# Gated attention and a squared-ReLU layer: w1 and the first inputs fetched by SyncE and GpSimd, half of the partitions each

## The chip, the cores and the metric

The kernel runs on one core of a Trainium2 chip. The metric is the device time of one execution in microseconds (us). A core has five engines with their own instruction streams: TensorE (PE in the profile; PEld is its weight load), VectorE (DVE), ScalarE (ACT), GpSimd (POOL) and SyncE (SP), which here does nothing but issue transfers. Transfers run on 16 DMA engines, whoever issues them. Before the change, SyncE issued all but six of the transfers of this kernel; those six were issued by ScalarE and none by GpSimd.

## The reference

```
# attention: q, k, v, a_re, a_im of shape (4, 8, 768, 48), f32
mag = sqrt(a_re**2 + a_im**2)
scale = minimum(mag, 0.999) / (mag + 1e-6)
a = (a_re + i a_im) * scale
for t in range(768):
    S = a[t][:, None] * S + outer(k[t], v[t])     # S complex, 48 x 48 for each batch and head
    y[t] = q[t] @ real(S)
# bridge: x = y as (3072 tokens, 384)
h = maximum(x @ w_in, 0)                          # w_in 384 x 2048
out = (h * h) @ w_out                             # w_out 2048 x 384
```

The two weights come as 64-bit floats. The kernel reads them as pairs of 32-bit words and makes 32-bit floats of them itself.

## The kernel before

The 768 steps of a sequence are cut into chunks of 128. A chunk of one sequence holds all 8 heads. Two sequences at the same chunk make a group, so there are 12 groups (0 to 11), six for each pair of sequences. For each group the kernel makes operands (gates, prefix products of the gates, keys and queries scaled by them), does the attention of both sequences with matrix products (`scores`, `sums_of_values`, `added`, `new_state`), brings the result into a token tile `x`, and runs the feed-forward layer over its 256 tokens (`first_product`, `squared_relu`, and the second product).

Features lie on the partitions: the even heads on partitions 0 to 63, the odd ones on 64 to 127, 48 features each. The 16 partitions that are left in each half hold the rows of the last two heads, three features side by side. So each load of q, k and the gates (`load_parts`, L487 to L501) goes half by half: for each of the two sequences and each half `hh` one transfer for the 48 rows (L493) and two or three small ones for the 16 rows (L501). The tile `raw` exists once. A group's load can start when the group before has no more use for it.

A load of a whole group is 16 transfers of 1.5 MB together. Group 0 alone is loaded in two parts: `l0.0` (the gates, 768 KB, half by SyncE and half by ScalarE), and `l0.1` (q and k, 768 KB, all by SyncE). `load_values` (`v`) fetches the values of a group in two transfers, 384 KB together.

The weight w1 is fetched in eight blocks of 256 columns (`fetch`, f0 to f7). A block is 768 KB in six transfers, because `w1_views` sets the rows of w1 to the same crossed order of partitions: in each half of the partitions two transfers for the 48 rows and one for the 16 rows (L617). The blocks of w2 (f8 to f15) are one transfer each (L613). The tile `words` has three buffers, so block i + 3 can't be fetched before block i has been decoded by VectorE (`weights`, D, L577 to L584 and a sum) and checked by ScalarE (`watch`, W, L590 and L592).

The order of all work is written out by hand in one long string, FRONT. A token is a letter and numbers: `l` loads the inputs of a group, `v` its values, `f` fetches a block of a weight, `D` decodes it, `W` checks it, `oG.K` is step K of the operands of group G, `aG.K` and `bG.K` are step K of the attention of its two sequences, `g` fills the rows of the token tile that the last heads belong to, `F`, `H` and the other capitals are the feed-forward layer, `s` stores. Every engine that is named in `by_hand` (L1173) executes its instructions in the order in which the tokens issue them. The string begins:

```
"l0.0 M0 v1 f0 v0 o0.0 l0.1 o0.3 o0.1 o0.4 o0.5 o0.7 o0.2 M1 D0 f1 o0.10 o0.8 o0.9 "
"o0.11 W0 o0.6 o0.12 o0.15 o0.22 f2 W1 o0.13 o0.16 o0.14 l1 W2 o0.17 D1 o0.18 f3 o0.19 "
"o0.20 o1.0 o1.6 a0.1 o1.3 o0.21 o1.1 D2 o1.2 a0.2 f4 a0.3 W3 D3 a0.0 a0.4 o1.4 o1.5 "
```

The operand steps that matter here, in the numbering of the list at L821: 0 `squares` (ACT L684, needs the tile `room`), 3 `sum_of_squares` (DVE L697), 6 `queries` (ACT L669, the first to need the loaded q), 7 `inverse` (DVE L715), 11 `gates` (DVE L735 and L739), 12 `negated` (ACT L743), 13 `grow` (DVE L755), 14 `keys` (ACT, the last to need `raw`), 15 and 16 the steps in blocks (DVE, `pr` and `ab` at L478), 19 `carried` (DVE, uses `room`), 20 `products` (DVE, writes `qk`), 21 `last_heads`. Most of VectorE's sums and products are recorded at L478, since a helper issues them.

`last_heads` copies the rows of the last two heads by six transfers (L815) into the tile `last`, and then GpSimd makes two small products (`prod`, L817 and L818) from it, which `new_state` (step 9 of the attention) uses on VectorE. Apart from the fills of tiles at the very start, these are all that GpSimd does.

Of the kernel before, what the change touches and what calls it, by code (L numbers as in the profile page):

```python
# [23 lines left out]
I32 = mybir.dt.int32  # L24
U32 = mybir.dt.uint32
AF = mybir.ActivationFunctionType
ALU = mybir.AluOpType
PSUM = bass.MemoryType.PSUM

P = 128  # L30
HH = 2
ROWS = 64
# [393 lines left out]
def quotient_path(ctx, tc, feat, vtok, w_in, w_out, w1, w2, out, n_seq, count):  # L426
# [49 lines left out]

    def tt(out, in0, in1, op):
        nc.vector.tensor_tensor(out=out, in0=in0, in1=in1, op=op)  # L478
# [8 lines left out]
    def load_parts(gi, part=None):  # L487

        parts = [slice(A_RE, Q), slice(Q, V), slice(A_RE, V)][2 if part is None else part]
        queues = nc.sync, (nc.scalar if part == 0 else nc.sync)  # L490
        for b, n in enumerate(groups[gi]):
            for hh, queue in enumerate(queues):
                queue.dma_start(  # L493
# [107 lines left out]
    def fetch(i):  # L601
        of_w2, j = block(i)
        f, fbs = slice(j * BLK, (j + 1) * BLK), slice(j * 2, (j + 1) * 2)
        if (w_out if of_w2 else w_in).dtype == F32:
            if of_w2:
                nc.sync.dma_start(out=w2[:, fbs], in_=w2_view(w_out)[:, fbs])
            else:
                for at, gs, src in w1_views(w_in, D, crossed=True):
                    nc.sync.dma_start(out=w1[at, gs, f], in_=src[:, :, f])
            return  # L610
        words = words_of[i] = dec.tile([P, E, 2], I32, name="words", bufs=3)
# [3 lines left out]
        else:  # L615
            for at, gs, src in w1_views(w_in, D, crossed=True):
                nc.sync.dma_start(  # L617
                    out=words[at].rearrange("p (g f) w -> p g (f w)", g=NG)[:, gs],
                    in_=src[:, :, f].bitcast(I32))
# [36 lines left out]
    operands = {}  # L656

    def make_operands(gi):
# [151 lines left out]
        def last_heads():  # L810
            for hh in range(HH):
                for g in range(NG):
# [4 lines left out]
            nc.gpsimd.tensor_copy(out=pd[:, now, :, NG], in_=last[gi % 2][:, 0:2, :, C])  # L817
            nc.gpsimd.tensor_scalar(out=pd[:, 0, :, NG], in0=last[gi % 2][:, IM, :, C], scalar1=-1.0,  # L818
                                    scalar2=None, op0=ALU.mult)
# [10 lines left out]
    def chunk(gi, b):  # L830
# [66 lines left out]
        def added():  # L897
            add = tiles["add"] = pm.tile([P, 2, NP, D], F32, tag="m", name="add")
            for c in (RE, IM):
                for p_ in range(NP):  # L900
                    for hh in range(HH):
                        rr, at = slice(hh * ROWS, (hh + 1) * ROWS), (HH * p_ + hh) * D
                        nc.tensor.matmul(add[rr, c, p_], lhsT=kt[c][:, p_, rr],  # L903
                                         rhs=v[:, at:at + D], start=True, stop=True)

# [114 lines left out]
    def outputs(i, r):  # L1020
# [30 lines left out]
        "l0.0 M0 v1 f0 v0 o0.0 l0.1 o0.3 o0.1 o0.4 o0.5 o0.7 o0.2 M1 D0 f1 o0.10 o0.8 o0.9 "  # L1051
        "o0.11 W0 o0.6 o0.12 o0.15 o0.22 f2 W1 o0.13 o0.16 o0.14 l1 W2 o0.17 D1 o0.18 f3 o0.19 "
        "o0.20 o1.0 o1.6 a0.1 o1.3 o0.21 o1.1 D2 o1.2 a0.2 f4 a0.3 W3 D3 a0.0 a0.4 o1.4 o1.5 "
        "a0.8 a0.5 a0.6 a0.9 a0.7 f5 b0.1 o1.7 W4 b0.0 D4 o1.10 o1.8 o1.9 b0.5 b0.2 b0.3 o1.11 "
        "W5 f6 b0.6 b0.4 b0.8 b0.7 g0 D5 o1.12 o1.22 v2 o1.13 W6 f7 F0.0 o1.15 o1.14 l2 F0.1 "
        "H0.0 o1.16 W7 F0.2 o1.17 H0.1 F0.3 H0.2 f8 D6 o1.18 F0.4 H0.3 o1.19 F0.5 H0.4 o2.6 "
        "F0.6 H0.5 o1.20 o2.0 f9 H0.6 W8 o2.3 o1.21 b0.9 o2.1 a1.1 D7 o2.2 a1.2 a1.3 W9 a1.0 D8 "
        "f10 a1.4 o2.4 o2.5 a1.8 F0.7 a1.5 a1.9 a1.6 H0.7 a1.7 f11 b1.1 D9 b1.0 b1.2 W10 b1.3 "
        "b1.4 b1.5 b1.8 D10 b1.6 b1.7 v3 T0.0 W11 g1 f12 b1.9 T0.1 D11 T0.2 F1.0 o2.7 W12 f13 "
        "D12 F1.1 H1.0 o2.10 F1.2 H1.1 o2.8 F1.3 H1.2 D13 f14 W13 F1.4 H1.3 T0.3 o2.9 o2.11 "  # L1060
        "F1.5 H1.4 f15 W14 D14 F1.6 o2.12 o2.22 T0.4 o2.13 W15 T0.5 o2.15 H1.5 T0.6 o2.14 H1.6 "
        "l3 o2.16 F1.7 T1.0 H1.7 o2.17 T1.1 D15 o2.18 T1.2 o2.19 T1.3 T0.7 o3.6 o2.20 o3.0 T1.4 "
        "E0.0 E0.1 s0.0 s0.1 o3.3 o3.1 a2.1 o2.21 T1.5 t0 o3.4 o3.2 t1 T1.6 o3.5 t2 a2.2 T1.7 "
        "o3.7 o3.10 a2.3 t3 E1.0 E1.1 s1.0 a2.0 o3.8 s1.1 o3.9 a2.5 a2.4 a2.6 o3.11 a2.8 a2.7 "
        "b2.0 a2.9 o3.12 o3.22 b2.1 b2.5 b2.2 b2.6 o3.15 b2.3 b2.7 b2.4 g2 b2.8 v4 o3.16 F2.0 "
        "o3.17 F2.4 H2.0 o3.13 o3.18 F2.1 H2.4 b2.9 o3.14 F2.5 H2.1 l4 X2.0 o3.19 F2.2 H2.5 "
        "F2.6 H2.2 X2.1 o3.20 F2.3 H2.6 F2.7 H2.3 X2.2 o3.21 Y2.0 Y2.1 Y2.2 Z2.0 H2.7 X2.3 o4.0 "
        "Y2.3 a3.1 o4.3 R2.0 Z2.1 o4.6 o4.4 o4.5 b3.0 Q2.2 Q2.1 Q2.3 o4.1 R2.1 Q2.0 o4.7 o4.2 "
        "Z2.2 b3.5 o4.10 o4.8 b3.6 Z2.3 R2.2 b3.7 o4.9 a3.0 o4.11 R2.3 a3.2 a3.3 Z2.4 a3.4 a3.5 "
        "o4.12 o4.22 o4.15 a3.8 a3.6 Z2.5 a3.7 g3 R2.4 o4.16 Z2.6 R2.5 o4.17 s2.0 F3.0 R2.6 "  # L1070
        "s2.1 a3.9 o4.18 F3.4 H3.0 o4.13 b3.1 H3.4 F3.1 b3.2 X3.0 o4.14 Y3.0 b3.3 F3.5 o4.19 "
        "H3.1 l5 b3.4 b3.8 H3.5 F3.2 X3.1 b3.9 F3.6 H3.2 v5 o4.20 F3.3 H3.6 F3.7 H3.3 X3.2 "
        "o4.21 Y3.2 Y3.1 o5.0 a4.1 Z3.0 o5.3 H3.7 X3.3 o5.4 Z3.1 R3.0 Y3.3 o5.6 o5.5 b4.0 Q3.1 "
        "Q3.0 Q3.3 o5.1 R3.1 Q3.2 o5.7 o5.2 Z3.2 a4.2 b4.5 o5.10 a4.3 R3.2 b4.6 a4.4 o5.8 a4.8 "
        "Z3.3 a4.9 b4.7 o5.9 a4.0 o5.11 R3.3 Z3.4 a4.5 o5.12 o5.22 o5.15 a4.6 b4.1 a4.7 Z3.5 "
        "b4.2 g4 R3.4 o5.16 b4.3 Z3.6 b4.4 R3.5 o5.17 s3.0 b4.8 R3.6 s3.1 F4.0 v6 b4.9 o5.18 "
        "F4.4 H4.0 o5.13 F4.1 H4.4 X4.0 o5.14 Y4.0 F4.5 o5.19 H4.1 l6 F4.2 H4.5 X4.1 F4.6 H4.2 "
        "o5.20 F4.3 H4.6 X4.2 o5.21 F4.7 H4.3 Y4.2 Y4.1 Z4.0 H4.7 X4.3 o6.0 Y4.3 b5.0 o6.3 R4.0 "
        "o6.6 o6.4 Z4.1 b5.5 o6.5 o6.7 o6.1 b5.6 o6.2 Q4.1 Z4.2 Q4.0 Q4.3 b5.7 R4.1 Q4.2 o6.10 "
        "o6.8 a5.0 R4.2 o6.9 Z4.3 a5.5 o6.11 a5.6 R4.3 Z4.4 a5.7 v7 o6.12 g5 o6.15 o6.22 Z4.5 "  # L1080
        "R4.4 Z4.6 R4.5 o6.16 s4.0 F5.0 R4.6 s4.1 o6.17 F5.4 H5.0 o6.13 o6.18 F5.1 H5.4 X5.0 "
        "o6.14 Y5.0 F5.5 o6.19 H5.1 l7 F5.2 H5.5 X5.1 F5.6 H5.2 o6.20 F5.3 H5.6 X5.2 o6.21 a6.1 "
        "H5.3 Y5.2 F5.7 Y5.1 a6.2 a6.3 H5.7 Z5.0 X5.3 o7.0 Y5.3 o7.3 a6.4 b6.0 R5.0 o7.4 o7.6 "
        "a6.8 b6.5 Z5.1 a6.9 o7.5 o7.1 o7.7 b6.6 o7.2 Q5.1 b6.1 Q5.0 Z5.2 Q5.3 b6.2 R5.1 b6.7 "
        "Q5.2 o7.10 a6.0 R5.2 o7.8 b6.3 a6.5 o7.9 Z5.3 o7.11 b6.4 a6.6 R5.3 b6.8 a6.7 g6 Z5.4 "
        "b6.9 o7.12 o7.22 v8 o7.15 Z5.5 F6.0 R5.4 R5.5 o7.16 s5.0 Z5.6 H6.0 o7.17 F6.4 R5.6 "
# [144 lines left out]
```

## Time and profile before

| | us |
|---|---|
| median of 6 runs | 707.78 |
| lowest and highest of them | 705.23, 708.21 |
| the profiled execution, its own time | 714.16 |
| span of its first to its last instruction | 712.4 |
| PE busy in the span | 632.2 (89%) |
| DVE busy | 523.9 (74%) |
| ACT busy | 380.7 (53%) |
| POOL busy | 14.2 (2%) |

The busy shares in 40 slices of 17.8 us each:

```
PE   0017959999989999999999999999999999999996
DVE  3899997979898697786695885975976963982130
ACT  6547683583646746646457458366366464250230
POOL 3000000000100000000000000000000000000000
DMA  6667843505207017026152160160170180010101
```

A digit is the busy share of a slice in tenths; 9 is 90% or more. The row DMA is the mean busy share of the 16 DMA engines. In the transfers SyncE is told as SPq and ScalarE's queue as ACTq: their rows show how long the issue took, and not how long the data took to arrive. The timeline tells for each instruction its start, its length, its engine, its line, the tiles, and in brackets how long the engine had been idle before it and what ended that. SyncE's issues in the first 92 us were these, in groups:

| from, us | what | how long its issues took, us |
|---|---|---|
| 0.79 | l0.0 (its half), v1 | 6.0 |
| 6.79 | f0 | 3.2 |
| 10.02 | v0 | 2.0 |
| 12.11 | l0.1 | 8.2 |
| 20.31 | f1, f2 | 6.5 |
| 31.66 | l1 | 8.8 |
| 40.54 | f3 | 3.8 |
| 48.75 | `last` of group 0 | 3.9 |
| 52.67 | f4, f5, f6 | 12.0 |
| 70.33 | token rows, v2 | 2.8 |
| 73.19 | f7 | 3.2 |
| 79.27 | l2 | 9.5 |
| 88.84 | f8, f9 | 2.4 |

### The profile page before, as it was taken

Reading aid. Unit: us, or ns where it says so; the run is one execution under the profiler, and the core shown is the slowest. Engines: PE = TensorE matmul, PEld = TensorE weight load, DVE = VectorE, ACT = ScalarE, POOL = GpSimd, SP = SyncE. Lnnn points to the kernel's source line nnn. Section 1 sums busy time; section 2 is a strip of 40 time slices with the busy share of each in tenths; the row PEclk is TensorE's granted clock in tenths of the full one; section 3 lists DMA queues with packets and bytes.
Section 4 is the critical chain, followed back from the end, with each engine's and each line's share of the span. In section 5 each row is a group of like instructions: output and inputs, shape, how many; then the busy total and the mean of one; then the engine's idle time right before and its main releaser. Section 6 shows DMA issues by size and latency. Waiting matters only on the chain.

```text
span 712.4 us, 12470 instructions
## 1 busy us (share of the span) xinstructions
PE 632.2 (89%) x4955; PEld 556.2 (78%) x4955; DVE 523.9 (74%) x916; ACT 380.7 (53%) x684; POOL 14.2 (2%) x49
## 2 busy tenths in 40 slices
PE   0017959999989999999999999999999999999996
PEld 0006747776669989998989989988989979989895
DVE  3899997979898697786695885975976963982130
ACT  6547683583646746646457458366366464250230
POOL 3000000000100000000000000000000000000000
PEclk9999777999999999999999999999999997999999
DMA  6667843505207017026152160160170180010101
GB/s 162 136 119 138 156 117 101 193 1 88 68 29 112 2 47 116 2 73 89 29 95 41 40 114 10 50 108 7 51 111 2 51 112 2 21 28 4 29 1 28
DMA packets 46148, 47.75 MB, mean 67 GB/s; under 512 B 6016, under 2 KB 40960, under 8 KB 46080
## 3 DMA queue, kind: packets, MB, share of 16 engines
q1 hardware_dynamic: 45600, 46.46, 33.3%
q8 instruction: 41, 0.67, 0.4%
q10 hardware_dynamic: 480, 0.39, 0.2%
q14 instruction: 27, 0.22, 0.1%
HBM read 36.18 MB, written 4.72 MB: 57 GB/s over the span
## 4 chain that ended last, share of the span: by engine, by line
PE 73%; DVE 12%; DMA 8%; ACT 2%; SPq 2%; issue 1%; DVEq 0%
PE h_ps L939 27%; PE o_ps L1016 24%; PE a_ps L859 6%; PE o_ps L955 6%; DMA raw<-in_feat_dram 5%; PE y L851 3%; PE y L885 3%; DVE pr L478 3%; PE add L903 3%; DVE ab L478 2%; PE tp L866 2%; SPq L815 2%; DMA words<-in_moe_w_in_dram 1%; DMA last<-qk 1%; DVE room L755 1%
## 5 line engine op out<-in xcount | busy, mean ns | idle before, releaser
L939 PE MATMUL h_ps<-x,w 128*128 128x256 f32 x1152 | 260.4, 386 | 2.7 <-DMA x<-x 2.7
L939 PEld LDWEIGHTS h_ps<-x,w 128*128 128x128 f32 x1152 | 221.6, 194 | 34.5 <-ACT room L751 1.6
L944 ACT ACTIVATE h<-h_ps 128x512 f32<-128x512 f32 x96 | 57.4, 598 | 130.4 <-PE h_ps L939 127.6
L1016 PE MATMUL o_ps<-w,h 128*128 128x192 f32 x640 | 112.7, 333 | 0.0
L1016 PEld LDWEIGHTS o_ps<-w,h 128*128 128x128 f32 x640 | 105.7, 193 | 1.7 <-issue 0.5
L478 DVE TENSOR_TENSOR a<-a_ps,mask 128x1024 f32<-128x1024 f32 x24 | 29.4, 1223 | 59.8 <-PE a_ps L859 59.5
L478 DVE TENSOR_TENSOR pr<-ab 128x384 f32<-128x384 f32 (+2 forms) x168 | 66.4, 413 | 6.1 <-ACT ab L743 1.8
L866 PE MATMUL tp<-ident,qk 128*128 128x128 f32 x120 | 22.7, 301 | 49.6 <-DVE qk L478 34.7
L945 ACT ACTIVATE h<-h 128x512 f32<-128x512 f32 x96 | 60.6, 631 | 3.0
L866 PEld LDWEIGHTS tp<-ident,qk 128*128 128x128 f32 x120 | 14.7, 150 | 56.2 <-issue 36.6
L1016 PE MATMUL o_ps<-w_sum,mix 128*128 128x192 f32 x320 | 56.0, 329 | 0.0
L1016 PEld LDWEIGHTS o_ps<-w_sum,mix 128*128 128x128 f32 x320 | 51.6, 190 | 1.1 <-issue 0.5
L478 DVE TENSOR_TENSOR mix<-h 128x256 f32<-128x256 f32 x40 | 16.8, 421 | 48.2 <-ACT h L945 48.0
L478 DVE TENSOR_TENSOR ab<-pr 128x192 f32<-128x192 f32 (+1 forms) x180 | 45.8, 276 | 4.6
L478 DVE TENSOR_TENSOR qk<-ab,qk 128x768 f32<-128x768 f32 x48 | 44.9, 956 | 0.9
L859 PE MATMUL a_ps<-qk 48*128 48x128 f32 x576 | 42.6, 299 | 0.0
L955 PE MATMUL o_ps<-w,h 128*128 128x384 f32 x128 | 42.2, 487 | 0.3 <-ACT x L894 0.3
L669 ACT ACTIVATE qk<-raw 128x768 f32<-128x768 f32 x24 | 36.8, 1535 | 10.2 <-DMA raw<-in_feat_dram 6.1
L859 PEld LDWEIGHTS a_ps<-qk 48*128 48x128 f32 x576 | 37.7, 205 | 4.8 <-issue 4.5
L669 ACT ACTIVATE ab<-raw 128x768 f32<-128x768 f32 x24 | 35.7, 1572 | 2.7 <-DVE qk L478 2.7
L955 PEld LDWEIGHTS o_ps<-w,h 128*128 128x128 f32 x128 | 24.2, 190 | 16.3 <-ACT x L894 0.5
L669 ACT ACTIVATE room<-z 128x768 f32<-128x768 f32 x24 | 36.6, 1558 | 0.0
(103 smaller groups left out, 793.9 us busy)
## 6 DMA issues: line engine op xcount, KB each, us to landing
raw<-in_feat_dram SPq DMA_DIRECT2D x44, 288.0 KB
words<-in_moe_w_out_dram SPq DMA_DIRECT2D x8, 768.0 KB
last<-qk SPq DMA_DIRECT2D x72, 64.5 KB
vt<-in_vtok_dram SPq DMA_DIRECT2D x24, 192.0 KB
out_dram<-o SPq DMA_DIRECT2D x24, 192.0 KB
raw<-in_feat_dram SPq DMA_DIRECT2D x132, 32.0 KB
words<-in_moe_w_in_dram SPq DMA_DIRECT2D x16, 192.0 KB
words<-in_moe_w_in_dram SPq DMA_DIRECT2D x32, 96.0 KB
```

The source lines that it names most:

```text
L478: nc.vector.tensor_tensor(out=out, in0=in0, in1=in1, op=op)
L669: nc.scalar.activation(out=out.rearrange("p c j n -> p c n j"), func=AF.Copy, in_=in_.rearrange("p c (n j) -> p c n j", j=L), **kwargs)
L851: nc.tensor.matmul(ys[p_ % 2][crossed(hh, p_), p_ // 2], lhsT=states[b][1 - c_seq % 2][rows(hh), c, p_], rhs=operand(c, p_, rows(hh)), sta ...
L859: nc.tensor.matmul(ps[:, hh, p_], lhsT=operand(2 + c, p_, rows(hh)), rhs=operand(c, p_, rows(hh)), start=(c == RE), stop=(c == IM))
L866: nc.tensor.transpose(tp[:, g], operands[gi][:, 2 + c, b, g, 0:C], ident)
L885: nc.tensor.matmul(tiles["y"][p_ % 2][crossed(hh, p_), p_ // 2], lhsT=v[:, at:at + ROWS], rhs=tiles["am"][:, hh, p_], start=(first and p_ ...
L903: nc.tensor.matmul(add[rr, c, p_], lhsT=kt[c][:, p_, rr], rhs=v[:, at:at + D], start=True, stop=True)
L939: nc.tensor.matmul(ps[:, j], lhsT=w1[:, g, (2 * f + j) * P:(2 * f + j + 1) * P], rhs=x_of[i][:, g], start=(g == 0), stop=(g == NG - 1))
L944: nc.scalar.activation(out=h, in_=h_ps[i, f], func=AF.Relu)
L945: nc.scalar.activation(out=h, in_=h, func=AF.Square)
L955: nc.tensor.matmul(o_of[i, b], lhsT=tokens_of(i, f, b)[:, j], rhs=w2[:, k], start=(k == 0), stop=(k == NFB - 1))
L1016: nc.tensor.matmul(to, lhsT=x(k)[:, j], rhs=factor(z)[:, 2 * k + j], start=(z in (0, 1, 3) and k == j == 0), stop=(k == KH // 2 - 1 and j ...
```

## The change

The loads of groups 0, 1 and 2 and the eight blocks of w1 are split between two queues. SyncE issues the transfers into partitions 0 to 63, GpSimd those into partitions 64 to 127. The half of `l0.0` that ScalarE issued stays with ScalarE. From group 3 on SyncE issues everything, as before, and w2 is fetched as before. No transfer is changed in size or shape.

Two new tokens stand for the second halves: `j` for that of a block, directly behind each `f`, and `i` for that of a load, directly behind `l0.1`, `l1` and `l2`. The order of the old tokens is the same. GpSimd joins the engines whose order is by hand. Its two products with `last` are taken out of `last_heads` (step 21 of the operands) and issued in the first `added` (step 8 of the attention) of the group.

On the built programs, the instructions of TensorE, VectorE and ScalarE are the same and stand in the same order. SyncE loses 46 issues, GpSimd gains 46. On GpSimd they stand in this order: f0, l0.1, f1, f2, l1, f3, f4 (second halves), the products of group 0, then f5, f6, f7, l2, the products of group 1, and then the products of the other groups.

```diff
+    other = nc.gpsimd
...
-    def load_parts(gi, part=None):
+    TWO_QUEUES = 3
+
+    def load_parts(gi, part=None, second=False):
         parts = [slice(A_RE, Q), slice(Q, V), slice(A_RE, V)][2 if part is None else part]
-        queues = nc.sync, (nc.scalar if part == 0 else nc.sync)
+        queues = [nc.sync, nc.scalar if part == 0 else other if gi < TWO_QUEUES else nc.sync]
+        if part != 0 and gi < TWO_QUEUES:
+            queues[not second] = None
         for b, n in enumerate(groups[gi]):
             for hh, queue in enumerate(queues):
+                if queue is None:
+                    continue
                 queue.dma_start(
...
-    def fetch(i):
+    def fetch(i, second=False):
...
-        words = words_of[i] = dec.tile([P, E, 2], I32, name="words", bufs=3)
+        if i not in words_of:
+            words_of[i] = dec.tile([P, E, 2], I32, name="words", bufs=3)
+        words = words_of[i]
...
             for at, gs, src in w1_views(w_in, D, crossed=True):
-                nc.sync.dma_start(
+                if (at.start >= ROWS) != second:
+                    continue
+                (other if second else nc.sync).dma_start(
                     out=words[at].rearrange("p (g f) w -> p g (f w)", g=NG)[:, gs],
                     in_=src[:, :, f].bitcast(I32))
...
-            nc.gpsimd.tensor_copy(out=pd[:, now, :, NG], in_=last[gi % 2][:, 0:2, :, C])
-            nc.gpsimd.tensor_scalar(out=pd[:, 0, :, NG], in0=last[gi % 2][:, IM, :, C], scalar1=-1.0,
-                                    scalar2=None, op0=ALU.mult)
...
         def added():
+            if gi not in products_of:
+                products_of.add(gi)
+                last_products()
...
+        def last_products():
+            pd, end = prod[gi % 2], last[gi % 2][:, 0:2, :, C]
+            nc.gpsimd.tensor_copy(out=pd[:, 1:3, :, NG], in_=end)
+            nc.gpsimd.tensor_scalar(out=pd[:, 0, :, NG], in0=end[:, IM], scalar1=-1.0,
+                                    scalar2=None, op0=ALU.mult)
...
-        "l0.0 M0 v1 f0 v0 o0.0 l0.1 o0.3 o0.1 o0.4 o0.5 o0.7 o0.2 M1 D0 f1 o0.10 o0.8 o0.9 "
-        "o0.11 W0 o0.6 o0.12 o0.15 o0.22 f2 W1 o0.13 o0.16 o0.14 l1 W2 o0.17 D1 o0.18 f3 o0.19 "
+        "l0.0 M0 v1 f0 j0 v0 o0.0 l0.1 i0.1 o0.3 o0.1 o0.4 o0.5 o0.7 o0.2 M1 D0 f1 j1 o0.10 "
+        "o0.8 o0.9 o0.11 W0 o0.6 o0.12 o0.15 o0.22 f2 j2 W1 o0.13 o0.16 o0.14 l1 i1 W2 o0.17 D1 "
+        "o0.18 f3 j3 o0.19 o0.20 o1.0 o1.6 a0.1 o1.3 o0.21 o1.1 D2 o1.2 a0.2 f4 j4 a0.3 W3 D3 "
...
+        "j": lambda i: fetch(i, True),
+        "i": lambda gi, part=None: load_parts(gi, part, True),
...
-               mybir.EngineType.Activation}
+               mybir.EngineType.Activation, mybir.EngineType.Pool}
```

## The prediction

> **What bounds the kernel now.** I read the busy shares in 40 slices first. PE is at 9 nearly everywhere from the fifth slice on, while DVE is at 8 to 9 from the second to the seventh. So the kernel has a front of about 105 us, in which VectorE sets the pace, and a long tail, in which TensorE does. The change touches transfers of the front only (its last one, the load of group 2, goes out at 79 to 89 us).
>
> Second, time by stretches, to see whether VectorE leaves room in the front (columns: stretch, its length, then busy us of PE, PEld, DVE, ACT, POOL with instruction counts, TensorE clock, DMA share, GB/s).
>
> ```profile
> 0.00:15.00 15.00, 0.48 (x1) 0.18 (x1) 3.59 (x9) 8.56 (x11) 6.80 (x25) 1.00 0.62 154
> 15.00:50.00 35.00, 0.87 (x3) 0.50 (x3) 32.76 (x54) 18.46 (x30) 0.00 (x0) 1.00 0.68 137
> 50.00:75.00 25.00, 16.81 (x173) 14.28 (x174) 24.34 (x30) 19.82 (x40) 0.42 (x2) 0.87 0.69 126
> 75.00:105.00 30.00, 21.39 (x87) 17.11 (x86) 28.82 (x52) 21.32 (x37) 0.00 (x0) 0.84 0.72 147
> ```
>
> The reader is to see that DVE is busy 32.76 of 35, 24.34 of 25 and 28.82 of 30 us: after 15 us there is next to nothing to win from an earlier transfer, except in single gaps. GpSimd (POOL) is empty from 7.44 us on.
>
> Third, the timeline of the first 24 us, for those gaps (start, length, engine, line, operation, tile; in brackets the idle time before it and what ended it).
>
> ```profile
> 14.83 0.56 DVE L577 TENSOR_SCALAR decoded<-words 128x768 int32<-128x768 int32 x1 [0.97 <-DMA raw<-in_feat_dram]
> ...
> 21.41 1.51 ACT L669 ACTIVATE qk<-raw 128x768 f32<-128x768 f32 x1 [1.64 <-DMA raw<-in_feat_dram]
> 22.73 0.75 ACT L743 ACTIVATE ab<-ab 128x672 f32<-128x672 f32 x1
> 23.52 0.56 DVE L478 TENSOR_TENSOR pr<-ab 128x384 f32<-128x384 f32 x1 [1.03 <-ACT ab L743]
> ```
>
> DVE loses 0.97 us until the first block of w1 (f0) has landed, and 1.03 us because the negation L743 stands on ScalarE behind the copy of q and k's raw rows (L669), which waits until 21.41 us for the second load of group 0 (l0.1). These are the two waits that the change could shorten. All that VectorE does from 23.52 to 100 us follows without a comparable gap, and what it does at 100 us (products) releases TensorE at 102 us. A shift at 23.52 us is therefore a shift of the end.
>
> Fourth, the DMA columns in short stretches.
>
> ```profile
> 7.50:10.00 2.50, 0.00 (x0) 0.00 (x0) 0.96 (x1) 2.50 (x2) 0.00 (x0) 1.00 0.80 220
> 10.00:12.50 2.50, 0.00 (x0) 0.00 (x0) 0.59 (x1) 2.47 (x5) 0.00 (x0) 1.00 0.94 185
> ...
> 17.50:20.00 2.50, 0.00 (x0) 0.00 (x0) 2.43 (x4) 2.24 (x5) 0.00 (x0) 1.00 0.33 85
> 20.00:22.50 2.50, 0.00 (x0) 0.00 (x0) 2.49 (x2) 1.09 (x1) 0.00 (x0) 1.00 0.50 158
> ...
> 25.00:27.50 2.50, 0.00 (x0) 0.00 (x0) 2.33 (x7) 0.20 (x1) 0.00 (x0) 1.00 1.08 179
> ```
>
> Where SyncE keeps transfers coming, the 16 DMA engines are full (share 0.94 to 1.08) at 179 to 185 GB/s. Only from 17.5 to 22.5 us do they idle.
>
> **The change part by part.** *The issues.* SyncE loses 24 of its 48 issues for w1 (L617, median 0.43 us), 6 for l0.1 and 8 each for l1 and l2; GpSimd gains as many. No row shows a transfer issued by GpSimd. From below its price is SyncE's quickest issue of the same words, 0.32 us; from above GpSimd's longest instruction, 1.73 us (L818 at 188.31 us, beside a VectorE operation of 1.75 us; alone it takes 0.21). Neither is near, so I take their middle, 1.03 us. The saving on SyncE itself I cost at nothing, with its covers: l1 waits for the keys' copy (ACT, done at 31.63 us; SyncE starts at 31.66), the rows of `last` for VectorE's products (48.6), `x` for ACT (70.3), l2 for ACT at 79.24. Without these covers it would be up to 46 issues of 0.43 us, some 20 us.
>
> *f0.* VectorE can start its decoding at 13.86 us at the earliest (L715 ends), so 0.97 us is the most to be had. It buys nothing alone: it only widens the gap before 23.52 us, whose end is set by l0.1. If GpSimd's half is late (7.44 us, its last memset, plus three issues of 1.73, plus 1.15 us, the time from l0.1's last issue at 20.26 us to 21.41) it lands at 13.8, still in time.
>
> *l0.1.* With both halves early, ACT is free at 19.78 us, copies until 21.3, negates (VectorE's factor is there at 21.6 less the 0.9 won at f0, so at 20.7) until 22.05: VectorE starts 1.47 us earlier than at 23.52. That is the cap of the gain. But a new competitor appears. Today SyncE's order sends l0.1 ahead of f1 and f2. GpSimd's queue isn't bound to that order: with 1.03 us an issue it has sent its halves of f0 and l0.1 by 7.44 + 9 x 1.03 = 16.7 us and goes straight on to f1 and f2, which VectorE doesn't decode before 36 us, while SyncE's half of l0.1 still stands behind the values v0. In bytes: until 8.5 us (first GpSimd issue done) 2.5 x (37 + 229 + 76) = 855 KB and 1.0 x 220 = 220 KB have moved. SyncE's queue then has 1283 KB to go until its half of l0.1 is through (786 + 4 x 393, less 1075). If full DMA engines share 185 GB/s evenly between two queues (an assumption; no row shows it), that takes 1283 / 92.5 = 13.9 us, to 22.4 us: 1.0 us **later** than 21.41. Ends: at 220 GB/s (the 7.5 to 10 us row) 20.2 us, a gain of 1.2; at 158 (the 27.5 to 30 us stretch) 24.7, a loss of 3.3. At 1.73 us an issue GpSimd's own half lands at 7.44 + 15.6 + 1.15 = 24.2, a loss of 2.8. I take +1.0.
>
> *VectorE beside GpSimd.* L577 and L581 take 0.55 to 0.56 us in each decoding; the two that met a GpSimd instruction, at 106.64 and 55.14 us, took 0.60 and 0.61. There are 16 in the eight decodings of w1, over which GpSimd issues. At 0.05 us: +0.8 us. From below 0; from above 0.21 us each, the whole of a short GpSimd instruction: 3.4. I take the measured 0.05.
>
> *l1, l2, f1 to f7.* l1's squares on ACT (44.78 us) start when VectorE gives up their tile (43.19 + 1.56 = 44.75), and VectorE needs them at 48.52 us, so l1 may land up to 47 us. GpSimd's eight issues end at 31.66 + 8 x 1.03 = 39.9, even at 1.73 at 45.5 plus 1.15. Cost 0; without that cover each us late would be one. l2 lands near 91.8 and its squares wait for VectorE until 96.3: 0. The waits of ACT on words (2.55 us at 27.30, 0.80 at 81.13) hold up no VectorE operation: 0.
>
> *The products with `last`* (two GpSimd operations of 0.2 us a group) move from the `last_heads` step to the first `added` step. On GpSimd's queue they now stand behind f4 in group 0 and behind l2 in group 1, and f5 behind the former. The `last` rows landed at 54.9 us and VectorE uses the products at 58.8; l2 is sent by 79.3 + 8.2 = 87.5, before 106.28: 0.
>
> The sum is 1.0 + 0.8 = +1.8 us. On the profiled execution (714.16 us with a span of 712.4, itself 6.4 above the median of the runs) that is 716.0; on the median of 707.78 it is **709.6**.
>
> Two rules speak to this. The Trainium skill, "DMA: Bandwidth & Descriptors", section "Rules for kernel authors", says not to bother with two transfers to disjoint partition halves, since both spray over the same 16 engines. The rows at 17.5 to 22.5 us (share 0.33 and 0.50) contradict it for that stretch; by the rule l0.1 would gain nothing, and the sum would be 0.8 us.
> "SBUF — State Buffer", section "SBUF: two separate sides", says that a transfer issued from GpSimd needs its descriptors written by it, which some VectorE operations lock out: 620 ns alone, about 3100 beside one. No run here shows it; by the larger figure nine issues would make l0.1 some 15 us late (an estimate from that page).
>
> **Rivals.** *Faster: the DMA engines are packed and l0.1 is in by 19.8 us.* For it: the idle share from 17.5 to 22.5 us. Against: f1 and f2 fill just that hole. It needs two queues to move over 220 GB/s, or GpSimd to take 1.2 to 1.3 us an issue, so that f1 comes later. Price: the cap, -1.47, so 706.3 us. It decides on the other side as soon as the copy of q starts before 21.41 us.
> *No change: hidden anyway.* The halves land as late as the wholes and VectorE's 0.05 us are lost in its pipeline: 707.8. For it: shares near 1.0 wherever transfers are many. Against: the order of the bytes does change.
> *Slow GpSimd.* Issues of 1.73 us, held by the VectorE that is never idle: 2.8 + 0.8 = +3.6, so 711.4, and further if they take longer. For it: the COPY at 187.60 us took 0.75 instead of 0.19 beside VectorE. Against: most GpSimd operations of the trace did not stretch.
>
> **How the numbers follow.** Forecast 0.43, faster 0.27, no change 0.14, slow GpSimd 0.16. Changes within 0.2% (1.4 us) can't be told from none. The cap of the gain lies just beyond this, so of the faster rival I count 0.22 as faster and 0.05 as same, and 0.03 of the no-change rival as faster. The forecast spans about +0.5 to +3.5: 0.37 slower, 0.06 same. Faster 0.25, same 0.22, slower 0.53. The range goes from 706.0 (the cap, with 0.3 for spread) to 713.0 (slow GpSimd and 1.6 more). For the slower cases alone it is 708.3 to 713.0.
>
> **What would show it.** ACT's copy of q and k raw rows (21.41 us now) near 22.4, VectorE's first step operation (23.52) near 24.5; GpSimd issues near 1 us; L577 and L581 longer on average up to 75 us; the squares of group 1 still directly after VectorE's release of their tile. The forecast is wrong if the copy of q starts before 21.4 us, or if the shift at 24 us isn't found again at 105 us.

## The result and the profile after

| | before | changed |
|---|---|---|
| median, us | 707.92 (77 runs) | 711.43 (35 runs) |
| lowest and highest, us | 704.82, 713.20 | 707.45, 716.10 |
| ratio to before | | 1.0048, 95% interval 1.0037 to 1.0060 |
| profiled execution, its own time and span, us | 714.16, 712.4 | 709.04, 707.3 |

The change made the kernel slower by 0.48%, some 3.4 us (2.6 to 4.2). The two profiled executions stand the other way round, and the first thing to learn here is why: that of before was above all its timed runs, that of the changed kernel near its lowest. Totals of two single profiles tell nothing of half a per cent; what follows compares them stage by stage.

The timeline of the changed kernel up to 26 us has the lines that answer to the four of the prediction (the numbers of the lines have moved: L577 is L587, L669 is L685, L743 is L759, L478 is L480):

```profile
17.06 0.56 DVE L587 TENSOR_SCALAR decoded<-words 128x768 int32<-128x768 int32 x1 [3.57 <-DMA raw<-in_feat_dram]
...
23.24 1.52 ACT L685 ACTIVATE qk<-raw 128x768 f32<-128x768 f32 x1 [3.94 <-DMA raw<-in_feat_dram]
24.56 0.76 ACT L759 ACTIVATE ab<-ab 128x672 f32<-128x672 f32 x1
25.35 0.56 DVE L480 TENSOR_TENSOR pr<-ab 128x384 f32<-128x384 f32 x1 [0.64 <-ACT ab L759]
```

Both waits that the change could have shortened are longer: VectorE starts on f0 2.23 us later (17.06 for 14.83, 3.57 us idle for 0.97), ScalarE copies q 1.83 us later (23.24 for 21.41), and the first block step is 1.83 us later (25.35 for 23.52).

The DMA engines weren't idle meanwhile. Time by stretches of the changed kernel (the last two columns are the DMA share and GB/s):

```profile
7.50:10.00 2.50, 0.00 (x0) 0.00 (x0) 0.96 (x1) 2.50 (x3) 2.50 (x5) 1.00 0.89 222
10.00:12.50 2.50, 0.00 (x0) 0.00 (x0) 0.96 (x1) 2.47 (x4) 1.85 (x4) 1.00 1.09 208
...
15.00:17.50 2.50, 0.00 (x0) 0.00 (x0) 0.44 (x1) 2.50 (x3) 0.60 (x2) 1.00 1.05 186
17.50:20.00 2.50, 0.00 (x0) 0.00 (x0) 2.40 (x4) 1.77 (x4) 1.39 (x4) 1.00 0.76 176
20.00:22.50 2.50, 0.00 (x0) 0.00 (x0) 2.43 (x4) 0.00 (x0) 0.93 (x2) 1.00 0.97 192
...
27.50:30.00 2.50, 0.00 (x0) 0.00 (x0) 2.40 (x5) 1.78 (x3) 0.00 (x0) 1.00 0.17 46
```

The hole of before from 17.5 to 22.5 us (share 0.33 and 0.50) is filled (0.76 and 0.97), and a hole has come up behind, from 27.5 us on. So more bytes were moved by 22.5 us than before, and yet those that the engines waited for came later. Which bytes went first is seen in the issues of GpSimd and SyncE (start, length; x is the number of issues; in brackets the idle time before them):

```profile
7.38 1.81 POOL L633 DMA_DIRECT2D words<-in_moe_w_in_dram  x3
9.18 0.60 POOL L503 DMA_DIRECT2D raw<-in_feat_dram  x1
...
11.33 0.52 POOL L511 DMA_DIRECT2D raw<-in_feat_dram  x1
13.80 0.51 POOL L511 DMA_DIRECT2D raw<-in_feat_dram  x1 [1.95 <-DMA words<-in_moe_w_in_dram]
14.69 0.57 POOL L633 DMA_DIRECT2D words<-in_moe_w_in_dram  x1 [0.38 <-DMA words<-in_moe_w_in_dram]
```

```profile
9.97 1.45 SPq L511 DMA_DIRECT2D raw<-in_feat_dram  x2
11.80 0.32 SPq L503 DMA_DIRECT2D raw<-in_feat_dram  x1
12.16 2.24 SPq L511 DMA_DIRECT2D raw<-in_feat_dram  x2
16.47 7.09 SPq L633 DMA_DIRECT2D words<-in_moe_w_in_dram  x6
```

GpSimd had sent its halves of f0 by 9.19 us and begins on f1 at 14.69. Both halves of l0.1 had been sent by 14.40 us. Before, SyncE's last issues for l0.1 ended at 20.26 us:

```profile
19.07 1.19 SPq L501 DMA_DIRECT2D raw<-in_feat_dram  x2
```

The data were **ordered 5.9 us earlier and arrived 1.8 us later**. The DMA view of the stretch from 6 to 27 us gives, for GpSimd's transfers, the median time from issue to landing (last column, us):

```profile
words<-in_moe_w_in_dram POOLq DMA_DIRECT2D x3, 192.0 KB, 6.9
words<-in_moe_w_in_dram POOLq DMA_DIRECT2D x6, 96.0 KB, 6.9
raw<-in_feat_dram POOLq DMA_DIRECT2D x2, 144.0 KB, 9.4
...
raw<-in_feat_dram POOLq DMA_DIRECT2D x4, 24.0 KB, 9.0
```

Even 24 KB take 9 us to land. At that length an issue's own 0.5 us says little of when its data come.

Behind the front, the timeline of TensorE has the first products with the state of group 0, before and in the changed kernel:

```profile
105.11 1.32 PE L851 MATMUL y<-qk,state 48*64 48x128 f32 x17
```

```profile
106.92 1.33 PE L864 MATMUL y<-qk,state 48*64 48x128 f32 x17
...
114.70 3.56 PE L961 MATMUL h_ps<-x,w 128*128 128x256 f32 x12
```

They are 1.81 us late: what was lost at 25 us is still there 80 us on. The products with w1 behind them took 4.54 us before and 3.56 now, since in both profiles TensorE is granted 0.50 of its clock from 100 to 115 us and all of it from 117.5 us on, and the kernel that comes later has less of its work in the slow stretch. 1 us is given back so in this execution (in the second profile of the changed kernel, below, they took 4.38 us, and little is). Put side by side in their order, VectorE's operations at 129 us are 0.85, 1.31 and 1.37 us late in the three profiles of the changed kernel.

Then the clock takes over. Granted TensorE clock from 585 to 600 us (the column before the last two), in the kernel before and in the changed one:

```profile
585.00:600.00 15.00, 13.37 (x122) 12.18 (x117) 7.61 (x13) 6.55 (x9) 0.37 (x2) 0.66 0.06 10
```

```profile
585.00:600.00 15.00, 14.79 (x198) 13.56 (x199) 7.92 (x15) 10.85 (x16) 0.37 (x2) 1.00 0.01 2
```

The profiled execution of before ran at 0.66 there and fell some 5.9 us behind the changed one's between 555 and 617 us, by VectorE's operations, in work that the change doesn't touch. That is why its total is the larger.

### The profile page after: what moved, and what is told of

It reads as the page before. It is cut to its first block, busy times and chain, and to the rows that moved or that the text cites. A ratio compares the mean times of both kernels' runs of the same rounds, so it can differ in the third digit from the quotient of the medians.

```text
span 707.3 us, 12514 instructions
## 1 busy us (share of the span) xinstructions
PE 624.7 (88%) x4955; PEld 550.5 (78%) x4955; DVE 523.7 (74%) x916; ACT 380.9 (54%) x684; POOL 37.7 (5%) x91
## 4 chain that ended last, share of the span: by engine, by line
PE 82%; DVE 9%; DMA 4%; ACT 2%; issue 1%; SPq 1%; POOL 0%; DVEq 0%; ACTq 0%
PE h_ps L961 33%; PE o_ps L1038 26%; PE a_ps L872 6%; PE o_ps L977 6%; PE y L864 3%; DMA raw<-in_feat_dram 3%; PE y L898 3%; PE add L919 2%; PE tp L879 2%; DVE ab L480 1%; DMA words<-in_moe_w_in_dram 1%; DVE room L480 1%; DVE decoded L589 1%; DVE decoded L594 1%; DVE pr L480 1%
## 5 line engine op out<-in xcount | busy, mean ns | idle before, releaser
L961 PE MATMUL h_ps<-x,w 128*128 128x256 f32 x1152 | 256.7, 382 | 4.2 <-ACT size L600 1.7
L961 PEld LDWEIGHTS h_ps<-x,w 128*128 128x128 f32 x1152 | 218.9, 191 | 35.0 <-issue 2.2
L1038 PE MATMUL o_ps<-w,h 128*128 128x192 f32 x640 | 110.6, 329 | 0.0
L1038 PEld LDWEIGHTS o_ps<-w,h 128*128 128x128 f32 x640 | 103.6, 190 | 1.6 <-issue 0.5
L480 DVE TENSOR_TENSOR pr<-ab 128x384 f32<-128x384 f32 (+2 forms) x168 | 66.4, 413 | 5.7 <-ACT ab L759 1.4
L480 DVE TENSOR_TENSOR a<-a_ps,mask 128x1024 f32<-128x1024 f32 x24 | 29.4, 1224 | 53.5 <-PE a_ps L872 53.2
L480 DVE TENSOR_TENSOR mix<-h 128x256 f32<-128x256 f32 x40 | 16.8, 421 | 47.1 <-ACT h L967 46.9
L480 DVE TENSOR_TENSOR ab<-pr 128x192 f32<-128x192 f32 (+1 forms) x180 | 45.8, 276 | 4.6
L480 DVE TENSOR_TENSOR qk<-ab,qk 128x768 f32<-128x768 f32 x48 | 44.9, 956 | 0.9
L685 ACT ACTIVATE qk<-raw 128x768 f32<-128x768 f32 x24 | 36.9, 1536 | 13.7 <-DMA raw<-in_feat_dram 7.6
L685 ACT ACTIVATE ab<-raw 128x768 f32<-128x768 f32 x24 | 35.7, 1576 | 2.6 <-DVE qk L480 2.6
L977 PEld LDWEIGHTS o_ps<-w,h 128*128 128x128 f32 x128 | 24.2, 190 | 16.3 <-ACT x L907 0.5
L685 ACT ACTIVATE room<-z 128x768 f32<-128x768 f32 x24 | 36.5, 1553 | 0.0
```

What stands on the lines that cost most here:

```text
L685: nc.scalar.activation(out=out.rearrange("p c j n -> p c n j"), func=AF.Copy, in_=in_.rearrange("p c (n j) -> p c n j", j=L), **kwargs)
L961: nc.tensor.matmul(ps[:, j], lhsT=w1[:, g, (2 * f + j) * P:(2 * f + j + 1) * P], rhs=x_of[i][:, g], start=(g == 0), stop=(g == NG - 1))
L977: nc.tensor.matmul(o_of[i, b], lhsT=tokens_of(i, f, b)[:, j], rhs=w2[:, k], start=(k == 0), stop=(k == NFB - 1))
L1038: nc.tensor.matmul(to, lhsT=x(k)[:, j], rhs=factor(z)[:, 2 * k + j], start=(z in (0, 1, 3) and k == j == 0), stop=(k == KH // 2 - 1 and j ...
```

## The experiments

Three theories stood against each other: that the order of the bytes decides (O), that GpSimd's issues themselves cost the time (G), and that the moved products with `last` do (P). The second halves of which blocks and loads GpSimd issues was made a choice by two sets:

```diff
+    SPLIT_F, SPLIT_L = set(range(8)), {0, 1, 2}
...
+        split = part != 0 and gi in SPLIT_L
...
+                if i in SPLIT_F and (at.start >= ROWS) != second:
+                    continue
```

**e1_products.** Every transfer by SyncE again; only the two products moved and GpSimd's order by hand are left.

```diff
-    SPLIT_F, SPLIT_L = set(range(8)), {0, 1, 2}
+    SPLIT_F, SPLIT_L = set(), set()
```

> Only the two GpSimd products of each group are moved (and GpSimd's order is by hand); every transfer is issued as before by SyncE. Theory O (the order of the bytes: GpSimd's queue runs ahead of SyncE's order, and f1 and f2 take DMA time from f0 and l0.1): nothing changes, within 0.15% of before, VectorE's decoding of f0 starts near 14.8 us and its first block step near 23.5. Rival P (the moved products delay later groups; they'd explain what the 3.5 us have beyond the 1.8 us seen at 24 us): 1 to 2 us slower than before, and GpSimd's products of a later group start later after their rows have landed than the 0.1 us of before.

708.23 us, ratio 1.0011 (0.9986 to 1.0036); first block step at 23.69 us. The times alone leave room for the 1 to 2 us of P, since the interval reaches 2.5 us. The trace doesn't: put side by side with those of before in their order, VectorE's operations start at most 0.26 us later anywhere up to 580 us (behind that the profile of before loses time by its clock). The moved products are not the cause: P is out.

**e2_later_ones.** Two queues only for the transfers behind the front: 31 issues by GpSimd instead of 46.

```diff
-    SPLIT_F, SPLIT_L = set(range(8)), {0, 1, 2}
+    SPLIT_F, SPLIT_L = {3, 4, 5, 6, 7}, {1, 2}
```

> f0, f1, f2 and l0.1 by SyncE alone as before; two queues only for f3 to f7, l1 and l2 (products moved). Theory O: the first 30 us are as before (decoding of f0 near 14.8, copy of q near 21.4, first block step near 23.5) and the later halves are hidden behind VectorE: within 0.15% of before. Rival G (issues by GpSimd cost time wherever they stand, by holding up VectorE or by splitting transfers): 1.5 to 3 us slower than before, as 30 of the 46 moved issues are left.

708.59 us, ratio 1.0004 (0.9985 to 1.0023); first block step at 23.75 us. 31 issues beside a busy VectorE cost nothing that can be measured: at most 1.6 us by the interval, where G had 1.5 to 3, and in the trace VectorE's operations from the first block step to 580 us start at most 0.44 us later than before. G is out as far as it speaks of every issue, and the later transfers are hidden, as costed.

**e3_hold.** All halves as in the changed kernel, but GpSimd first copies a few numbers of the loaded q and k, so it can't go on to f1 and f2 before l0.1 has landed.

```diff
     def fetch(i, second=False):
...
+        if second and i == 1:
+            nc.gpsimd.tensor_copy(out=held, in_=raw[:, Q:V, :, :, 0])
```

> All 46 issues by GpSimd as in the changed kernel, but GpSimd first makes a small copy that reads q and k of l0.1 and so waits for both halves before it goes on to f1 and f2. Theory O: f1 and f2 no longer compete, l0.1 lands at 18.5 to 20.5 us instead of 23.2, the first block step starts at 22.0 to 23.5 us: 0 to 1.5 us faster than before, 3 to 5 us faster than the changed kernel. If f0's lateness (17.1 us) comes from l0.1's halves and not from f1 and f2, the decoding of f0 stays near 17 us and the first block step comes at about 24.7, some 1.2 us slower than before. Rival G: no better than the changed kernel (3.5 us slower than before).

708.09 us, ratio 1.0000 (0.9977 to 1.0022). From its timeline, ScalarE, GpSimd and VectorE in turn:

```profile
21.40 1.52 ACT L694 ACTIVATE qk<-raw 128x768 f32<-128x768 f32 x1 [1.98 <-DMA raw<-in_feat_dram]
24.12 0.76 ACT L768 ACTIVATE ab<-ab 128x672 f32<-128x672 f32 x1 [1.19 <-DVE ab L480]
```

```profile
22.06 0.29 POOL L618 COPY held<-raw 128x12 f32<-128x12 f32 x1 [7.09 <-DMA raw<-in_feat_dram]
22.57 3.17 POOL L642 DMA_DIRECT2D words<-in_moe_w_in_dram  x6 [0.22 <-issue]
```

```profile
17.29 0.56 DVE L590 TENSOR_SCALAR decoded<-words 128x768 int32<-128x768 int32 x1 [3.66 <-DMA raw<-in_feat_dram]
```

With f1 and f2 held back until 22.57 us, l0.1 lands as before (copy of q at 21.40 for 21.41). But f0 is still late (17.29), and now the negation waits for VectorE (1.19 us) and not for the copy of q. The hold separates the two delays: l0.1 is late because of f1 and f2, and f0 is late without them. What still goes out earlier than before is GpSimd's own half of l0.1, sent directly behind its half of f0; that this is what delays f0 is argued, since no run takes it away alone. One of the two delays is enough to push the first block step, here to 24.91 us (+1.39). For a late f0 some 1.2 us of time were expected, which the interval (up to 1.6 us) doesn't exclude; still, a front as late as the changed kernel's at an unchanged time was odd, so it was run again.

**r_e3.** The same kernel.

> The kernel in which GpSimd waits for the second load of group 0 before it issues its halves of f1 and f2, unaltered, once more. Its first profile had the first block step 1.40 us later than before (the decoding of f0 at 17.29 us holds VectorE up, not the copy of q), as late as in the changed kernel, and yet its median was that of the kernel before (708.09 and 708.07 us). If the front decides, the first step is 1 to 2 us late again, and the median now lies 1 to 2 us above that of the kernel before. If holding f1 and f2 back takes something away that does not show in the front, the median is that of the kernel before again.

708.85 us beside 708.21, ratio 0.9997 (0.9969 to 1.0026); decoding of f0 at 16.30, copy of q at 21.27, first block step at 23.93 us, only 0.41 late. So the first profile showed a late execution of this kernel. Its front is 0.4 to 1.4 us late, and its time is that of before within 2 us either way.

**e4_f1_f2.** Only the second halves of f1 and f2 by GpSimd, six transfers of 768 KB together, which it sends at once.

```diff
-    SPLIT_F, SPLIT_L = set(range(8)), {0, 1, 2}
+    SPLIT_F, SPLIT_L = {1, 2}, set()
```

> Only the second halves of f1 and f2 by GpSimd, f0 and l0.1 and all later transfers by SyncE. GpSimd sends the six at once from 7.4 us on. Theory O: they take DMA time from f0 and l0.1, most of all the transfers that are wanted first: decoding of f0 at 16.5 to 19 us, copy of q after 22.5 us, 1.5 to 4 us slower than before, though only 6 issues moved. Rival G: 6 of 46 issues, so at most 0.5 us slower.

713.35 us, ratio 1.0082 (1.0054 to 1.0109). Its timeline, GpSimd, then VectorE, then ScalarE:

```profile
7.37 3.39 POOL L638 DMA_DIRECT2D words<-in_moe_w_in_dram  x6
```

```profile
29.14 0.56 DVE L480 TENSOR_TENSOR pr<-ab 128x384 f32<-128x384 f32 x1 [0.77 <-ACT ab L764]
```

```profile
27.02 1.53 ACT L690 ACTIVATE qk<-raw 128x768 f32<-128x768 f32 x1 [4.32 <-DMA raw<-in_feat_dram]
```

Six issues cost 5.8 us where 46 cost 3.4, and more than the 1.5 to 4 us expected. The number of issues is not what counts: these six move 768 KB that are wanted at 36 us and later ahead of l0.1, which slips by 5.61 us, although each of its own transfers is SyncE's as before. SyncE's small issues of l0.1 waited 5.4 us in all until `words` had landed, and its last ones ended at 25.86 us for 20.26. O holds, and neither G nor P can make this of so few issues.

**e5_values_late.** If the order of the bytes decides, it can be improved with one queue. The kernel before sends the values v1 and v0 (768 KB, wanted from 57 us on) ahead of l0.1; here they go behind f2.

```diff
-        "l0.0 M0 v1 f0 v0 o0.0 l0.1 o0.3 ... o0.22 f2 W1 "
+        "l0.0 M0 f0 o0.0 l0.1 o0.3 ... o0.22 f2 v0 v1 W1 "
```

> The kernel before, one queue, with the values of groups 1 and 0 (768 KB, needed from 57 us) moved from ahead of the second load of group 0 to behind f2. The theory that the order of the bytes decides: f0 is decoded at 13.9 us (14.83 before), the copy of q starts at about 19.8 us (21.41), the first block step at about 22.05 (23.52): up to 1.47 us faster than before, 0.2%. The rival, that the transfers are limited by SyncE's issues and not by what stands ahead of them: the copy of q at 21 us or later and no difference.

705.28 us (703.40 to 707.74) beside 707.68, ratio 0.9965 (0.9945 to 0.9985). Faster, by some 2.5 us. Its timeline:

```profile
13.46 0.55 DVE L577 TENSOR_SCALAR decoded<-words 128x768 int32<-128x768 int32 x1
```

```profile
19.35 1.51 ACT L669 ACTIVATE qk<-raw 128x768 f32<-128x768 f32 x1
```

Neither has a bracket: VectorE goes from L715 to f0 without a wait, and ScalarE from the check of f0 to the copy of q. The first block step is at 21.45 us, 2.07 earlier, where 1.47 was expected: ScalarE's check of f0 ahead of the copy began 0.33 us earlier in this execution (17.40 for 17.73), and the expectation added up lengths that overlap in the pipeline (the copy ends at 20.86, the negation starts at 20.67).

**e6_both.** The changed kernel with the same move of the values.

> The changed kernel with the values of groups 1 and 0 moved behind f2, on SyncE; GpSimd's halves as in the changed kernel. The theory that the order of the bytes decides: SyncE's half of the second load of group 0 no longer stands behind 768 KB of values while GpSimd's f1 and f2 take half of the engines, so f0 is decoded at 14 to 15 us (17.06), q copied at 20 us or earlier (23.24), the first block step near 22.1 (25.35): 3 us faster than the changed kernel and 0.5 to 1.5 faster than the kernel before. The rival, that transfers issued by GpSimd are slow in themselves (its half lands late whatever SyncE does): q copied at 23 us still, and a time like the changed kernel's, +0.4%.

708.85 us, ratio 1.0009 (0.9991 to 1.0027) to before; the changed kernel ran at 710.45 beside it. In its profile the front is as early as in e5 (f0 at 13.57, copy of q at 19.46, first block step at 21.56), so transfers by GpSimd aren't slow in themselves. But the time isn't e5's, nor the 0.5 to 1.5 us below the kernel before that were expected: 3.6 us are lost elsewhere. Two more profiles of the same kernel were taken to find them.

**r_e6 and r_e6_again.**

> The changed kernel with the values behind f2, unaltered, for a second profile. Its median was 708.85 us, though its profiled execution (705.49 us, its lowest of 12) has the first block step at 21.56 us, 1.96 us before that of the kernel before. If the arrival of GpSimd's halves differs from one execution to the next, an execution of 708 to 710 us shows the first block step at 23.5 to 25.5 us, behind f0 or the copy of q. If the 2 to 3 us are lost elsewhere, the first step is at 21.5 us again, and the loss stands in a later stretch.

> The same kernel a third time, since one execution tells little of a spread. The same two readings: the first block step at 23.5 to 25.5 us in a slower execution if the arrival varies, at 21.5 us if it does not.

709.85 and 706.49 us; first block step at 21.60 and 21.62 us. The front doesn't vary; the whole difference between these executions lies behind it. Time from 205 to 228 us in e6_both (705.49 us) and in r_e6:

```profile
205.00:228.00 23.00, 23.00 (x116) 20.73 (x115) 20.36 (x38) 15.03 (x27) 0.00 (x0) 1.00 0.59 86
```

```profile
205.00:228.00 23.00, 23.00 (x99) 19.85 (x99) 19.15 (x37) 11.35 (x23) 0.00 (x0) 0.90 0.55 83
```

TensorE is busy throughout in both, at 1.00 and 0.90 of its clock, with 116 and 99 products done. In the same stretch the kernel before had 0.93, the changed one 1.00. Each execution draws its own clock here. The 96 products with w1 that fill this stretch took 20.96 us in e6_both and 24.02 us in r_e6 (22.64 before, 20.96 in the changed kernel): the stretch is worth up to 3 us.

**r_after and r_after_again.** The changed kernel for a second and a third profile.

> The changed kernel once more, unaltered, for a second profile. Its first profiled execution (709.04 us) was one of its lowest and showed VectorE's first block step 1.83 us later than before (25.35 for 23.52), while the medians differ by 3.5 us. If the late arrival of the second load of group 0 is all there is, this profile shows the first step again at 25.0 to 25.7 us and TensorE's first products of the feed-forward layer near 107 us. If the arrival varies from one execution to the next (the rest of the 3.5 us), the first step is at another place, 26 to 28 us.

> The changed kernel, unaltered, for a third profile (the first two had the first block step at 25.35 and 24.94 us, in executions of 709.04 and 712.50 us). If the arrival varies, an execution of 711 us or more may show it at 26 us or later; if not, it is at 24.9 to 25.4 us again whatever the time.

710.45 us (10 runs), ratio 1.0035 (1.0013 to 1.0056), and a single 711.24 us. ScalarE and VectorE in the second profile:

```profile
22.32 1.54 ACT L685 ACTIVATE qk<-raw 128x768 f32<-128x768 f32 x1 [3.04 <-DMA raw<-in_feat_dram]
24.14 0.76 ACT L759 ACTIVATE ab<-ab 128x672 f32<-128x672 f32 x1 [0.28 <-DVE ab L480]
```

and in the third:

```profile
14.97 0.56 DVE L587 TENSOR_SCALAR decoded<-words 128x768 int32<-128x768 int32 x1 [0.80 <-DMA words<-in_moe_w_in_dram]
...
24.65 0.56 DVE L480 TENSOR_TENSOR pr<-ab 128x384 f32<-128x384 f32 x1 [2.01 <-ACT ab L759]
```

The two queues race, and the loser differs. In the second execution f0 was the late one (17.26 us; the negation waits for VectorE), in the third f0 was nearly in time and l0.1 alone was late (VectorE waits 2.01 us for the negation). The first block step is 1.83, 1.42 and 1.13 us late.

**e7_values_late_w0.** e5, with the check of f0 on ScalarE moved behind the copies and the negation.

```diff
-        "o0.11 W0 o0.6 o0.12 o0.15 o0.22 f2 v0 v1 W1 "
+        "o0.11 o0.6 o0.12 o0.15 o0.22 W0 f2 v0 v1 W1 "
```

> The kernel before with the values moved behind f2 and the check of block 0 of w1 on ScalarE moved behind the copies of q and the negation. The theory that the path is load, copy of q, negation, first step: with the check of block 0 out of ScalarE's way too, the copy of q starts as soon as the load lands (17 to 19 us), the first step at about 21.6 us: 1.9 us faster than before. If something else follows directly (VectorE itself is busy until 21 us), the gain is no more than that of moving the values alone, 1.5 us or less.

704.50 us (702.70 to 706.09), ratio 0.9956 (0.9938 to 0.9974): the fastest here, 3.1 us (1.8 to 4.4) below the kernel before and 6 us below the changed one. VectorE's first block step in its timeline:

```profile
21.38 0.56 DVE L478 TENSOR_TENSOR pr<-ab 128x384 f32<-128x384 f32 x1
```

No bracket any more (in e5 VectorE still waited 0.19 us for the negation). The load has landed by 17.56 us, when ScalarE copies q, and VectorE itself is what the step waits for. The step is 0.07 us earlier than in e5, so whether moving the check adds anything can't be told from these runs. The 3.1 us are more than the 1.9 expected; the front gives 2.14 of them.

All profiles side by side, us:

| kernel | f0 decoded | q copied | first block step | against before | ratio of times |
|---|---|---|---|---|---|
| before | 14.83 | 21.41 | 23.52 | | |
| changed | 17.06 | 23.24 | 25.35 | +1.83 | 1.0048 |
| r_after | 17.26 | 22.32 | 24.94 | +1.42 | 1.0035 |
| r_after_again | 14.97 | 22.57 | 24.65 | +1.13 | one time |
| e1_products | 15.08 | 21.58 | 23.69 | +0.17 | 1.0011 |
| e2_later_ones | 15.57 | 21.63 | 23.75 | +0.23 | 1.0004 |
| e3_hold | 17.29 | 21.40 | 24.91 | +1.39 | 1.0000 |
| r_e3 | 16.30 | 21.27 | 23.93 | +0.41 | 0.9997 |
| e4_f1_f2 | 20.71 | 27.02 | 29.14 | +5.62 | 1.0082 |
| e5_values_late | 13.46 | 19.35 | 21.45 | -2.07 | 0.9965 |
| e6_both | 13.57 | 19.46 | 21.56 | -1.96 | 1.0009 |
| r_e6, r_e6_again | 13.66, 13.83 | 19.49, 19.51 | 21.60, 21.62 | -1.92, -1.90 | one time each |
| e7_values_late_w0 | 13.60 | 17.56 | 21.38 | -2.14 | 0.9956 |

## Why the prediction was right, and where it was not

**The competitor was right, and nearly its size.** The prediction had GpSimd's queue go on to f1 and f2 while SyncE's half of l0.1 stands behind the values, and the DMA engines shared evenly: copy of q at 22.4 us. It came at 23.24, 22.32 and 22.57, on average 22.71 us (+1.30 for +1.0). e3 shows that f1 and f2 cause this, since with them held back the copy is at 21.40 and 21.27; e4 shows it with them alone. That the two queues shared the engines evenly is shown by no row. That the values stand ahead of l0.1 is the other half of it: with both queues and the values out of the way (e6) q is copied at 19.46.

**The shift is kept to the end of the front.** 1.83 us at 25 us and 1.81 at 105, in the second profile 1.42 and 1.42. So far this step holds. The prediction took it on to the end of the kernel, and there it isn't one to one: behind the stretch at half clock the shifts are 0.85, 1.31 and 1.37 us (at 129 us), and two places further on add to them (below).

**f0, costed at nothing, failed.** The prediction let GpSimd's half of f0 land at 13.8 us at the latest, from the length of its issues and 1.15 us behind the last. The issues were quicker than that, and the data of f0, f1 and f2 took 6.9 us at the median and not 1.15: full DMA engines, and not the issue, set when these landed. Nor was it true that f0 matters only for the gap ahead of 23.52 us. That holds for an earlier f0. A later one pushes VectorE's decoding and, behind it in VectorE's order, the product that the negation needs. In e3 this alone makes the first block step late, and in the second profile of the changed kernel it is the later of the two delays. In the sum it hides, because the two delays run side by side and only the longer counts: with either, the step is 1.1 to 1.8 us late, 1.46 on average over the three profiles.

**GpSimd's issues, 1.03 us, were mis-sized.** They took 0.51 to 0.60 us. Eight go out without a wait, and the ninth waits until one of its own has landed (1.95 us before 13.80). The time was bounded from an instruction of a different kind, and the middle of the bounds was farther off than the lower one (0.32). The rival of a slow GpSimd shows what a number alone is worth: its price, 711.4 us, is the measured median, and its issues of 1.73 us weren't there.

**VectorE beside GpSimd, +0.8 us, was mis-sized.** L587 and L591 take 0.55 or 0.56 us in 15 of the 16 cases, and 0.64 in one, at 56.98 us, where GpSimd computes a product; its counterpart took 0.61 before. Nothing is left of the term: from 25 to 108 us VectorE's operations are 1.81 to 1.87 us late throughout. The two lengthened ones of before had met GpSimd's arithmetic, and the prediction took them for what an issue does.

**The later transfers and the moved products cost nothing that can be told**, as costed: e2 and e1 with their traces. The squares of group 1 start directly behind VectorE's release of their tile, as they did:

```profile
46.74 1.48 ACT L700 ACTIVATE room<-raw 128x1536 f32<-128x1536 f32 x1 [7.88 <-DVE ab L480]
```

**What the terms don't hold.** The forecast of +1.8 us was made of +1.0 and +0.8; what the profiles show of these is +1.5 and nothing. The measured +3.4 us (2.6 to 4.2) is more than that by about 1.9 us, so the forecast came as near to the median as it did by a term that wasn't there. e6 says the same: its front is 1.9 us early in all three profiles, and its median is not below that of the kernel before. No such rest shows in e2, in e3 and its repetition, or in e4, whose 5.8 us are its front's 5.6.

The prediction put everything behind the front at nothing. The traces show two places there where all six profiles of the changed kernel and of e6 lose time, and none of the eight others. The first is the start of the feed-forward products at 205 us, before and in the changed kernel:

```profile
204.90 22.64 PE L939 MATMUL h_ps<-x,w 128*128 128x256 f32 x96 [1.17 <-DMA x<-x]
```

```profile
206.29 20.96 PE L961 MATMUL h_ps<-x,w 128*128 128x256 f32 x96 [1.73 <-DMA x<-x]
```

From SyncE's first issue of the token rows that they read to their start there pass 3.47 to 3.92 us in the six and 3.04 to 3.15 in the eight. The second place is the end. VectorE's last operation, before (span 712.4 us) and in the changed kernel (span 707.3 us):

```profile
702.82 0.36 DVE L478 TENSOR_TENSOR o<-o_ps,o 128x192 f32<-128x192 f32 x1 [2.19 <-PE o_ps L1016]
```

```profile
696.29 0.36 DVE L480 TENSOR_TENSOR o<-o_ps,o 128x192 f32<-128x192 f32 x1 [2.19 <-PE o_ps L1038]
```

From its end to the end of the span there pass 10.64 to 11.17 us in the six and 9.20 to 9.58 in the eight. Averaged over the three profiles of the changed kernel, this is 0.7 us in the first place and 1.5 in the second; with the front's 1.5 it makes 3.6, where 3.4 were measured. For e6 it is -1.9, 0.6 and 1.5, together +0.1, where the ratio gives +0.6 (-0.6 to 1.9). So the rest has its places. Why it is lost there stays open: SyncE issues the same transfers in the same order there as before, GpSimd's last transfer went out by 86 us, e3 makes the same 46 issues and loses nothing in either place, and what SyncE waits for at the end the trace doesn't tell.

The clock lies over this. In the stretch from 205 to 228 us it wins and loses up to 3 us from one profile to the next (20.96 and 24.02 us for the same products of one kernel). On average it is a small part: over the timed runs the mean granted clock was 0.9763 in e6 and 0.9776 in e5, and in the 35 runs of before beside them a clock lower by 0.001 goes with 0.27 us, so 0.35 of the 3.6 us between the two.

**The pages, against the runs.** The Trainium skill, "DMA: Bandwidth & Descriptors", section "Rules for kernel authors", says not to bother with two transfers to disjoint halves. It was right not to expect a gain, and it doesn't speak of the loss that the runs show: 0.48%, and 0.82% in e4. Its section "Issuing engines are not separate DMA queues" says that transfers of several engines interleave on the same 16 DMA engines; 6.9 to 9.4 us to landing, and l0.1 late by 5.61 us behind six transfers of another queue, agree with it. "SBUF — State Buffer", "SBUF: two separate sides", has two figures for a whole transfer by GpSimd, about 620 ns alone and 3100 beside a VectorE operation that locks GpSimd out. What can be set beside them here is the length of the issues, and these took 0.51 to 0.60 us while VectorE was busy for 2.33 of 2.50 us (32.5 to 35 us). No lock-out shows in them; whether VectorE ran an operation of the kind that the page means at those moments isn't known from these runs.

## What to carry to other kernels

A queue is not only a way to issue, it also decides which data come first. A second queue let what was wanted late overtake what was wanted soon here, with the DMA engines full (share 0.89 to 1.09 from 7.5 to 17.5 us); before splitting a load over two queues, list in order of bytes what else the second queue will send, and make it wait if that isn't wanted yet. Where a first load is late, look for bytes ahead of it that nobody needs: moving 768 KB of values back brought 2.5 us here, and the split cost 3.4. And set two profiles side by side operation by operation, to the very end: over half of this loss stood at 205 us and behind the last operation, in places that the prediction had at nothing.

## What was not expected of the hardware

GpSimd's transfers go in larger packets. By the page of the changed kernel (packets, MB, share of the engines' time):

```profile
q1 hardware_dynamic: 41408, 41.35, 30.0%
q0 software_dynamic: 2208, 5.11, 4.0%
```

That is 2.3 KB a packet for GpSimd's queue and 1.0 KB for SyncE's, over transfers of the same shapes among others; the engines' time for a MB is nearly the same (0.78% and 0.73% of their span).

The TensorE clock is worth about as much as the change. The same program took 705.49 and 709.85 us with first block steps 0.04 us apart, and in the stretch from 205 to 228 us the fourteen profiles were granted from 0.85 (r_after) to 1.00 of it.
